# Moving keys and Gram products forward in the first layer of a delta-rule and feed-forward kernel

## The chip, the cores and the metric

The kernel runs on one core of a Trainium2 chip. A core has a matrix engine (TensorE, PE in the profile; its weight loads are PEld), a vector engine (VectorE, DVE), a scalar engine (ScalarE, ACT), a general engine (GpSimd, POOL) and a queue engine (SyncE, SP), which here only issues DMA transfers. Each engine works through its own list of instructions in order and waits on semaphores for the others. The metric is the device time of one execution in microseconds.

## The reference

Two parts follow one another. The first is a delta rule over 768 tokens, for 4 batches of 8 heads with 48 dimensions: for each token

```
k_n   = k / (|k| + 1e-6)
y_t   = q_t . state                      (before the update)
v_old = state . k_t
state = state + beta_t * outer(k_t, v_t - v_old)
```

The second takes the outputs as 3072 rows `x` of 384 and computes

```
h = x @ w_in                             (384 to 2048)
g = max(h, 0) + alpha * min(h, 0)
out = g @ w_out                          (2048 to 384)
```

All of it is in 32-bit floating point. The inputs are q, k, v, beta, w_in, w_out and alpha; the only output is `out`.

## The kernel before

The 768 tokens are cut into 12 chunks of 64, and the 4 batches into 2 pairs. One chunk of one pair is a *step*; there are 24 steps, numbered 0 to 23, with two steps per chunk. A step holds 128 rows (2 batches of 64 tokens) and 8 heads. Within a chunk, the rule becomes matrix products: the products of all keys with one another (the *Gram* products, `grams`, L486), a triangular system, products with the state, and an update of the state. The triangular inverses of four steps are made together on DVE by an elimination (`eliminate`: four block transposes L540, one mask on POOL L555, then 30 steps of two instructions each, L565 and L571, and transposes back). `eliminate(1)` does this for steps 4 to 7, and can start when the four Gram products of these steps have been weighed (L494) and copied into one tile (`keep`, L529).

When both steps of a chunk are done, its 256 tokens go through the feed-forward part: `ffn_in` (L1075) multiplies by w_in, 48 products of 128x256 per chunk; six products make a pair of column blocks in one of two PSUM banks, which ACT (L1085) and DVE (L1087) then evict. `ffn_out` (L1118) multiplies by w_out. PE's whole list is written out by hand as an interleaving: `weave` deals out the steps of generators by their shares, `alongside(p, c)` puts p products of `ffn_in(0)` and c half conversions of weights between two pieces of the attention part.

The weights arrive as 32-bit words and are converted before use. Each piece takes two instructions on ACT (L240, L242), a shift on DVE (L256) and an addition on POOL or DVE (L263). w_in comes in 12 pieces of 512 KB, w_out in 16 pieces of 384 KB, through staging areas in tiles that have other uses later. `weights()` holds the bookkeeping: `fetch(n)` issues loads until n pieces have been issued; when a piece is finished, the conversion fetches one more. ACT begins the conversion of the next piece before the current one is finished. All loads go through SP's queue in the order of the program, together with the loads of keys, queries and values (L137, L175). A load into a tile waits in that queue until the readers of the tile are done.

`pause(n, upto)` (L1664) puts a one-element memset on POOL into a staging area, and then fetches: the load has to wait for the memset, and so for everything that POOL has in its list before it. Two such pauses delay parts of w_in.

In the first layer, steps 0 to 3 are handled specially. `first_chunk` does steps 0 and 1, with an elimination in small blocks. Before it, some matrix products whose results are not used (`busy`, L1539, 5.5 products of 128x512) stand in PE's list; they write a PSUM bank that was read just before by the copies of the masked query products (`a_t`, L1569 on ACT). `second_pair` then does steps 2 and 3: the products with the inverses (`own_values` and three calls of `one_round`, L857), the outputs (L930), and the state update (L946), woven with `ffn_in(0)`. In between, it prepares steps 4 to 7: `keys(k)` transposes the keys of step k on PE (L430), copies them (`k_t`, L439), squares and sums them (L386, L393), and issues the load of the keys three steps further, which reuses the tile; `weigh` makes the weights from the norms (L408, L409, L413, L419, L420); `grams` makes the Gram products.

For the state update, `copy_late(n)` keeps a second copy of the keys of steps 0 to 3 with the two batches swapped for odd heads, in three instructions (L153, L155) on POOL.

Numbers that the text uses: `BEGUN` is the number of pieces of `eliminate(1)` that are done within `second_pair`, `SOON` the number done in the next weave; the rest follows while `ffn_out(0)` runs.

Of the kernel before, what the change touches and what calls it, by code (L numbers as in the profile page):

```python
# [25 lines left out]
FP32 = mybir.dt.float32  # L26
# [17 lines left out]
def kernel(  # L44
# [11 lines left out]
    nc = tc.nc  # L56
# [8 lines left out]
    G = H // 2  # L65
# [38 lines left out]
    def half(i):  # L104
        return slice(64 * i, 64 * i + 64)
# [39 lines left out]
    def late_key(n):  # L145
        return late_keys.get(n, k_late[n % NKL])

    def copy_late(n):

        if n >= NKL:  # L150
            late_keys[n] = work.tile([128, DM], FP32, name="o_sb").rearrange("p (h d) -> p h d", h=H)
        src, dst = (x.rearrange("p (g a) d -> p a g d", a=2)[:, :, :, 0:D] for x in (early(n), late_key(n)))
        nc.gpsimd.tensor_copy(out=dst[:, 0], in_=src[:, 0])  # L153
        for t in range(2):
            nc.gpsimd.tensor_copy(out=dst[half(1 - t), 1], in_=src[half(t), 1])  # L155

    def load_q(n):
        if n < N:
# [2 lines left out]
    def load_v(n):  # L161
        if n < N:
            v_raw[n] = work.tile([128, H, D], FP32, name="v_raw", bufs=3)
            fetch(v, n, v_raw[n])
# [301 lines left out]
    def now(pieces):  # L466
        for x in pieces:
            x()
# [1193 lines left out]
    def pause(n, upto):  # L1662

        nc.gpsimd.memset(in_stages[n][0:1, 0:1].bitcast(FP32), 0.0)  # L1664
        fetch_in(upto)
# [3 lines left out]
    for f in range(FT // 2, FT, 2):  # L1669
        stages.append(w_out[:, f : f + 2].rearrange("p f d -> p (f d)").bitcast(U32))  # L1670
    ids = [0, 1, 2, 3, 4, 5, 6, 0, 1, 2, 6, 0, 1, 2, 0, 1]
    fetch_out, _, conv_out = weights(pieces, stages, ids, out_done, None, 5, 1)
    PARTS_OUT = 2 * len(pieces)

# [17 lines left out]
    def gram(n):  # L1692
        return grams(n, big[n % 3])

    for n in (0, 2, 3):
        copy_late(n)
    squared(0)
    copy_0 = key(0)
# [31 lines left out]
    first_weights(1)  # L1730
    for c in range(2):
        first_spread(c, quarter_weight, quarter_of, NQ4)
    copy_late(1)
    gram_3 = gram(3)
    pick(3, gram_3, 0)
    picks(2, gram_2)
# [9 lines left out]
    raw(2, gram_2)  # L1746
    raw(3, gram_3)
    nc.scalar.mul(minus, minus, -1.0)
    load_v(2)
    for n in range(1, NJ):  # L1750
        load_early(n + NKE)
    load_v(3)
    mask = queries(big[1])
    slopes()
    short(5, ps_one())
# [16 lines left out]
    def alongside(products, pieces, *gens):  # L1772
        gens = [(part(first_in, products), products), (part(convert_on, pieces), pieces), *gens]
        weave(*[x for x in gens if x[1] > 0])

    def second_pair():

        n, m, x = 2, 3, NJ
        both = (n, m)

        def burst(step, width):
            p = ps_big()
            pieces = []
            for i in range(2):
                pieces += step(n + i, p[:, :, i * width : (i + 1) * width])
            now(pieces)

        def keys(k):
            flip_more(k)
            squared(k)  # L1790
            norms(k)
            load_early(k + NKE)

        def through(i, p):
            now(through_state(i, None, p))

        now(next_state(0))
        scale_first(n)
        pause(8, 10)
        scale_first(m)  # L1800
        alongside(2, 2)
        now(next_state(1))
        keys(x)
        alongside(3, 3)
        burst(matrix, G * C)
        for i in both:
            turn_matrix(i, nc.gpsimd)
        now(weigh(x))
        alongside(3, 2)
        for i in both:  # L1810
            flips(N, i)
            load_q(i + 2)
        fetch_in(11)
        alongside(2, 1)
        keys(x + 1)
        fetch_in(12)
        alongside(2, 1)
        y = ps_big()
        through(n, y[:, :, 0 : G * D])
        alongside(2, 1)  # L1820
        through(m, y[:, :, G * D : 2 * G * D])
        now(weigh(x + 1))
        alongside(3, 2)
        burst(own_values, G * D)
        for i in both:
            turn_values(i, nc.gpsimd)
        fetch_out(1)
        alongside(3, 2)
        now(grams(x))
        alongside(2, 2)  # L1830
        burst(lambda i, p: one_round(i, 0, p), G * D)
        load_v(4)
        fetch_out(2)
        alongside(2, 1)
        keys(x + 2)
        fetch_out(3)
        alongside(2, 2)
        burst(lambda i, p: one_round(i, 1, p), G * D)
        now(weigh(x + 2))
        alongside(2, 1)  # L1840
        now(grams(x + 1))
        alongside(2, 1)
        burst(lambda i, p: one_round(i, 2, p), G * D)
        alongside(2, 1)
        keys(x + 3)
        fetch_out(4)
        alongside(2, 1)
        now(grams(x + 2))
        now(weigh(x + 3))
        alongside(2, 1)  # L1850
        burst(outputs, G * D)
        alongside(3, 2)
        now(grams(x + 3))
        alongside(2, 1)
        for i in both:
            to_ffn(i)
        squares(x + 4)
        alongside(2, 1, (part(blocks, 5), 5))
        for i in both:
            now(next_state(i))  # L1860
            load_late(i + 2)
            load_v(i + 3)
            alongside(2, 0)
        alongside(IN_PARTS - 45, 0)

    def flip_more(n):
        now(flipped(n, ps_one()))

    blocks, BEGUN, SOON, LAST = eliminate(1), 5, 9, 6
    second_pair()  # L1870
    weave(
        (part(conv_out, PARTS_OUT - 10 - LAST), PARTS_OUT - 10 - LAST), (ffn_in(1), IN_PARTS - 4),
# [166 lines left out]
```

## Time and profile before

| quantity | value |
|---|---|
| time, median of 3 runs | 653.72 us (652.72 to 653.98) |
| time of the profiled execution | 652.53 us |
| its span, first to last instruction | 650.8 us |
| DVE, ACT, POOL busy | 74%, 40%, 19% of the span |
| PE busy in 30 to 40, 40 to 50, 50 to 60 us | 8.35, 10.00, 8.62 us |
| PE busy in 60 to 70, 70 to 80, 80 to 90 us | 9.21, 10.00, 7.98 us |
| DMA engines' share in 50 to 60 us | 0.85 |

A row of the timeline gives the start, the duration, the engine, the line of the kernel, the operation, what it writes and reads, the sizes, and how many instructions were merged. In brackets stands how long the engine had been idle before it, and who released it; "issue" means that the profile shows nothing that it waited for. SPq rows are DMA issues; the transfer lands some microseconds later. In the chain of waits each row is a start, a duration and what took it.

### The profile page before, as it was taken

The page shows a single profiled execution, that of the slowest core. Times are in us where ns is not written, and L with a number is a line of the kernel's source. Part 1 is how long each engine was busy: PE and PEld are TensorE (multiplying, and loading weights), DVE is VectorE, ACT ScalarE, POOL GpSimd, SP SyncE. Part 2 cuts the span into 40 slices and gives each one's busy share as a digit, 9 for nine tenths or more (in the row PEclk, how much of TensorE's full clock was granted, in tenths as well). Part 3 has the DMA queues.
Part 4 walks back from the last instruction along what each step waited for, and adds up shares of the span by engine and source line. Part 5 has one row for each costly group of instructions (what it writes and reads, how often), then busy time and mean ns, then how long its engine had stood idle before and what let it go on. Part 6 is the DMA issues. An engine that isn't in the chain of part 4 may idle for free.

```text
span 650.8 us, 21349 instructions
## 1 busy us (share of the span) xinstructions
PE 633.3 (97%) x9157; PEld 559.0 (86%) x9157; DVE 483.4 (74%) x1157; ACT 258.2 (40%) x605; POOL 126.0 (19%) x250
## 2 busy tenths in 40 slices
PE   6998989999999999999999999999999999999997
PEld 5676777566789989989989989989999999999997
DVE  5857698978998788577678568678868568477383
ACT  6676565154645153154145144033145154042240
POOL 7296511010001000000000010000044053062350
PEclk9999999999999999999999999999999999999999
DMA  8856764013412320211211111121121210100000
GB/s 159 223 166 146 195 163 108 12 39 63 84 30 39 69 40 19 56 40 32 46 30 26 39 39 26 35 42 25 39 44 21 50 26 2 38 3 3 24 1 25
DMA packets 106798, 36.88 MB, mean 57 GB/s; under 512 B 99872, under 2 KB 103088, under 8 KB 106704
## 3 DMA queue, kind: packets, MB, share of 16 engines
q1 hardware_dynamic: 104832, 35.03, 24.2%
q8 instruction: 72, 1.18, 0.7%
q10 hardware_dynamic: 1872, 0.49, 0.4%
q14 instruction: 22, 0.18, 0.1%
HBM read 30.78 MB, written 4.72 MB: 55 GB/s over the span
## 4 chain that ended last, share of the span: by engine, by line
PE 85%; DVE 6%; DMA 3%; ACT 3%; issue 1%; SPq 1%; POOL 0%; ACTq 0%
PE p_ffn L1075 22%; PE p_ffn L1140 17%; PE p_more L1392 8%; PE p_more L1308 5%; PE p_ffn L1118 4%; PE p_ffn L1298 3%; PE p_ffn L1392 3%; PE p_ffn L1303 2%; PE p_pair L807 2%; PE p_pair L430 2%; PE p_pair L747 2%; PE p_pair L930 2%; PE p_pair L917 2%; PE p_pair L795 1%; PE p_pair L486 1%
## 5 line engine op out<-in xcount | busy, mean ns | idle before, releaser
L1075 PE MATMUL p_ffn<-xt,w_in 128*128 128x256 f32 x768 | 178.1, 384 | 2.6 <-DVE act L1087 2.4
L1075 PEld LDWEIGHTS p_ffn<-xt,w_in 128*128 128x128 f32 x768 | 141.7, 190 | 23.4 <-ACT space_out L242 2.3
L1087 DVE SCALAR_TENSOR_TENSOR act<-act,al_t,p_ffn 128x256 f32<-128x256 f32 x112 | 48.6, 475 | 22.7 <-ACT act L1085 22.5
L1085 ACT ACTIVATE act<-p_ffn 128x512 f32<-128x512 f32 x56 | 33.3, 595 | 79.8 <-PE p_ffn L1075 79.6
L1332 POOL TENSOR_TENSOR k_t<-k_t 128x128 f32<-128x128 f32 (+1 forms) x48 | 29.3, 610 | 167.2 <-ACT k_t L1327 164.7
L571 DVE TENSOR_TENSOR block<-block,prod 128x30 f32<-128x30 f32 (+9 forms) x150 | 49.9, 332 | 5.2
L419 POOL TENSOR_TENSOR beta_t<-beta_t,rec 128x8 f32<-128x8 f32 x20 | 5.1, 257 | 237.6 <-DVE rec L413 228.0
L565 DVE TENSOR_TENSOR prod<-block 128x30 f32<-128x30 f32 (+9 forms) x150 | 48.8, 325 | 2.8 <-POOL block L555 1.4
L1140 PE MATMUL p_ffn<-w_out,act 128*128 128x192 f32 x288 | 49.6, 328 | 0.0
L1140 PEld LDWEIGHTS p_ffn<-w_out,act 128*128 128x128 f32 x288 | 46.6, 190 | 0.3
L973 ACT COPY xt<-p_pair 128x384 f32<-128x384 f32 x22 | 10.4, 478 | 90.7 <-PE p_pair L969 76.9
L1332 POOL TENSOR_TENSOR block<-block 128x128 f32<-128x128 f32 (+1 forms) x48 | 27.9, 582 | 16.9 <-ACT block L1327 14.4
L1298 PE MATMUL p_ffn<-xt,w_in 128*128 128x256 f32 x96 | 28.7, 381 | 0.5 <-DVE o_sb L1160 0.5
L759 ACT COPY inv<-p_pair 32x256 f32<-32x256 f32 x40 | 14.5, 361 | 24.9 <-DVE u L921 24.1
L1160 DVE TENSOR_TENSOR o_sb<-u,p_ffn 128x192 f32<-128x192 f32 x24 | 7.9, 351 | 20.8 <-PE p_ffn L1140 20.0
L1346 DVE SCALAR_TENSOR_TENSOR act<-block,al_t,act 128x256 f32<-128x256 f32 x32 | 19.1, 637 | 5.3 <-ACT block L1342 5.3
L799 ACT COPY y<-p_pair 128x384 f32<-128x384 f32 x22 | 10.6, 480 | 30.8 <-PE p_pair L795 29.2
L825 DVE TENSOR_TENSOR r<-v_raw,p_pair 64x192 f32<-64x192 f32 (+1 forms) x60 | 21.1, 352 | 1.0
L1392 PE MATMUL p_more<-w_out,act 128*128 128x192 f32 x128 | 21.8, 329 | 0.0
L1327 ACT COPY k_t<-p_more 128x512 f32<-128x512 f32 x16 | 9.4, 586 | 31.4 <-PE p_more L1308 26.7
L1346 DVE SCALAR_TENSOR_TENSOR act<-k_t,al_t,act 128x256 f32<-128x256 f32 x32 | 21.7, 718 | 0.1
L807 PE MATMUL p_pair<-beside,k_t 48*64 48x112 f32 x704 | 21.4, 259 | 0.2 <-ACT beside L458 0.2
(287 smaller groups left out, 1409.0 us busy)
## 6 DMA issues: line engine op xcount, KB each, us to landing
v_raw<-in_v_dram SPq DMA_DIRECT2D x48, 96.0 KB, 2.9
qp<-in_q_dram SPq DMA_DIRECT2D x48, 96.0 KB, 3.0
out_dram<-o_sb SPq DMA_DIRECT2D x90, 48.0 KB, 1.6
space_out<-in_moe_w_out_dram SPq DMA_DIRECT2D x11, 384.0 KB, 3.9
ke<-in_k_dram SPq DMA_DIRECT2D x43, 96.0 KB, 3.1
kl<-in_k_dram SPq DMA_DIRECT2D x80, 48.0 KB, 2.6
w_out<-in_moe_w_in_dram SPq DMA_DIRECT2D x6, 512.0 KB, 7.6
w_out<-in_moe_w_out_dram SPq DMA_DIRECT2D x5, 384.0 KB, 6.0
```

Source lines behind the costliest of these rows:

```text
L565: nc.vector.tensor_tensor(out=prod, in0=r[:, 0:j, j : j + 1].to_broadcast([128, j, n]), in1=r[:, j : j + 1, j + 1 : HB].to_broadcast([128, ...
L571: nc.vector.tensor_tensor(out=r[:, 0:j, j + 1 : HB], in0=r[:, 0:j, j + 1 : HB], in1=prod, op=ALU.add)
L807: nc.tensor.matmul(p[half(t ^ a), a, g], k_t[n][dims(a), g, half(t)], beside[bp][dims(a), t, g])
L1075: nc.tensor.matmul(p_h[:, i], w_in[:, t, (f + i) * 128 : (f + i + 1) * 128], xt[:, t], start=(t == 0), stop=(t == KT - 1),)
L1085: nc.scalar.activation(g, p_h, ACT.Relu, scale=-1.0)
L1087: nc.vector.scalar_tensor_tensor(out=g[:, i], in0=g[:, i], scalar=al_t[:, f + i : f + i + 1], in1=p_h[:, i], op0=ALU.mult, op1=ALU.add,)
L1140: nc.tensor.matmul(p, x(i), w(i), start=(i == 0), stop=(i == FP - 1))
L1298: nc.tensor.matmul(p[:, f * 256 : f * 256 + 256], w(2, f), xt[:, 2], start=True, stop=False)
L1308: nc.tensor.matmul(q[:, j], a, b, start=True, stop=True)
L1332: nc.gpsimd.tensor_tensor(out=dst, in0=a, in1=b, op=ALU.add)
L1346: nc.vector.scalar_tensor_tensor(out=g[:, f], in0=r[:, f], scalar=al_t[:, 2 * i + f : 2 * i + f + 1], in1=g[:, f], op0=ALU.mult, op1=ALU.add,)
L1392: nc.tensor.matmul(p, x(i), w(i), start=(i == 0), stop=(i == FP - 1))
```

## The change

Six things change, all in the first 90 us.

- The second copies of keys 3 and 1 are made by ACT, after the sign change of `minus` and ahead of the copies of a_t. Those of 0 and 2 stay on POOL.
- As a consequence, the loads of keys 5 and 6 go ahead of the load of key 4, which follows the values of step 3.
- The second pause of w_in fetches up to 11 pieces instead of 10, and the last piece (12) is fetched where the 11th was.
- In `second_pair`, the Gram products of steps 4 to 7 and `keys` of steps 6 and 7 stand one or two stages earlier in PE's list, each stage being `own_values`, a round, or the outputs. The number of ffn products between them changes so that the total is the same.
- The loads of w_out's pieces start later: the first two are issued after the weights of step 6, behind a third pause (`pause_out`).
- Twelve pieces of `eliminate(1)` are done in `second_pair` instead of five, in four places, the first of them ahead of the outputs. `SOON` goes from 9 to 8.

```diff
-    def copy_late(n):
+    def copy_late(n, engine=nc.gpsimd):
...
-        nc.gpsimd.tensor_copy(out=dst[:, 0], in_=src[:, 0])
+        copy_by(engine, dst[:, 0], src[:, 0])
         for t in range(2):
-            nc.gpsimd.tensor_copy(out=dst[half(1 - t), 1], in_=src[half(t), 1])
+            copy_by(engine, dst[half(1 - t), 1], src[half(t), 1])
...
+    out_stages = stages
+    def pause_out(n, upto):
+        nc.gpsimd.memset(out_stages[n][0:1, 0:1].bitcast(FP32), 0.0)
+        fetch_out(upto)
...
-    for n in (0, 2, 3):
+    for n in (0, 2):
         copy_late(n)
...
-    copy_late(1)
     gram_3 = gram(3)
...
     nc.scalar.mul(minus, minus, -1.0)
+    for n in (3, 1):
+        copy_late(n, nc.scalar)
     load_v(2)
-    for n in range(1, NJ):
+    for n in (2, 3):
         load_early(n + NKE)
     load_v(3)
+    load_early(1 + NKE)
...
-        pause(8, 10)
+        pause(8, 11)
...
-        fetch_in(11)
+        fetch_in(12)
         alongside(2, 1)
         keys(x + 1)
-        fetch_in(12)
...
         now(weigh(x + 1))
-        alongside(3, 2)
+        alongside(2, 1)
+        now(grams(x))
+        alongside(2, 2)
         burst(own_values, G * D)
         for i in both:
             turn_values(i, nc.gpsimd)
-        fetch_out(1)
-        alongside(3, 2)
-        now(grams(x))
+        alongside(2, 1)
+        keys(x + 2)
+        alongside(2, 2)
+        now(grams(x + 1))
         alongside(2, 2)
         burst(lambda i, p: one_round(i, 0, p), G * D)
+        now(weigh(x + 2))
+        pause_out(0, 2)
         load_v(4)
-        fetch_out(2)
         alongside(2, 1)
-        keys(x + 2)
+        keys(x + 3)
+        alongside(2, 1)
+        now(grams(x + 2))
+        alongside(2, 1)
+        burst(lambda i, p: one_round(i, 1, p), G * D)
+        now(weigh(x + 3))
         fetch_out(3)
-        alongside(2, 2)
-        burst(lambda i, p: one_round(i, 1, p), G * D)
-        now(weigh(x + 2))
         alongside(2, 1)
-        now(grams(x + 1))
+        now(grams(x + 3))
         alongside(2, 1)
         burst(lambda i, p: one_round(i, 2, p), G * D)
-        alongside(2, 1)
-        keys(x + 3)
         fetch_out(4)
-        alongside(2, 1)
-        now(grams(x + 2))
-        now(weigh(x + 3))
-        alongside(2, 1)
+        alongside(3, 2, (part(blocks, 4), 4))
         burst(outputs, G * D)
-        alongside(3, 2)
-        now(grams(x + 3))
-        alongside(2, 1)
+        alongside(4, 3, (part(blocks, 1), 1))
         for i in both:
             to_ffn(i)
         squares(x + 4)
-        alongside(2, 1, (part(blocks, 5), 5))
+        alongside(2, 1, (part(blocks, 3), 3))
         for i in both:
             now(next_state(i))
             load_late(i + 2)
             load_v(i + 3)
-            alongside(2, 0)
-        alongside(IN_PARTS - 45, 0)
+            alongside(2, 0, (part(blocks, 2), 2))
+        alongside(IN_PARTS - 47, 0)
...
-    blocks, BEGUN, SOON, LAST = eliminate(1), 5, 9, 6
+    blocks, BEGUN, SOON, LAST = eliminate(1), 12, 8, 6
```

In `second_pair`, `x` is 4, so `keys(x + 2)` belongs to step 6 and `grams(x)` to step 4.

## The prediction

> **What bounds the kernel now.** First the page: TensorE (PE) is busy for 97% of the span, so time is won or lost only where PE sits idle, or where its order is held back.
>
> ```profile
> span 650.8 us, 21349 instructions
> PE 633.3 (97%) x9157; PEld 559.0 (86%) x9157; DVE 483.4 (74%) x1157; ACT 258.2 (40%) x605; POOL 126.0 (19%) x250
> ```
>
> Second, the waits of PE up to 200 us, because the diff ends at about 90 us and PE's order after that is unchanged. Two of them lie inside the edited stretch:
>
> ```profile
> PE p_pair L857 <- issue: 2.4, 3, 1.4
> PE p_ffn L1075 <- DVE act L1087: 2.4, 2, 1.9
> ```
>
> Third, the timeline of PE where they are. The first two stop in the middle of a burst, with no releaser; the third waits for VectorE (DVE), whose transposes and state updates (rows below it) are queued ahead of the eviction L1087.
>
> ```profile
> 54.59 0.56 PE L857 MATMUL p_pair<-r,diag 64*64 64x48 f32 x24 [0.79 <-issue]
> 60.79 0.26 PE L857 MATMUL p_pair<-sums 64*64 64x48 f32 x2 [1.38 <-issue]
> 87.00 5.42 PE L1075 MATMUL p_ffn<-xt,w_in 128*128 128x256 f32 x24 [1.92 <-DVE act L1087]
> ...
> 81.58 2.31 DVE L540 STREAM_TRANSPOSE block<-same 128x256 f32<-128x256 f32 x4
> 83.76 2.20 DVE L954 TENSOR_TENSOR beside<-beside,p_pair 48x384 f32<-48x384 f32 x4
> 85.98 0.87 DVE L1087 SCALAR_TENSOR_TENSOR act<-act,al_t,p_ffn 128x256 f32<-128x256 f32 x2
> ```
>
> Fourth, ScalarE (ACT) in the same stretch. Its queue is in order, and a conversion whose w_out piece has not landed (L240) stops all behind it:
>
> ```profile
> 63.10 0.54 ACT L386 ACTIVATE ksq<-ke 128x384 f32<-128x384 f32 x1
> 63.53 0.57 ACT L240 ACTIVATE w_out<-space_out 128x384 uint32<-128x384 uint32 x1
> ...
> 68.75 0.56 ACT L240 ACTIVATE w_out<-space_out 128x384 uint32<-128x384 uint32 x1 [2.76 <-DMA space_out<-in_moe_w_out_dram]
> 69.22 0.59 ACT L1085 ACTIVATE act<-p_ffn 128x512 f32<-128x512 f32 x1
> ...
> 78.54 0.56 ACT L240 ACTIVATE w_out<-w_out 128x384 uint32<-128x384 uint32 x1 [3.97 <-DMA w_out<-in_moe_w_out_dram]
> ```
>
> Fifth, the chain: a piece that stands behind a key load on the queue of SyncE (SP) lands 3.74 us after its issue.
>
> ```profile
> 64.31 0.63 SPq L137
> ...
> 64.99 3.74 DMA space_out<-in_moe_w_out_dram
> ```
>
> Before, these waits hit ACT while PE had other work. Last, the start, where `busy` keeps PE waiting for ACT's two copies of a_t:
>
> ```profile
> 19.18 1.12 ACT L1569 COPY a_t<-p_pair 128x512 f32<-128x512 f32 x2
> 20.35 7.39 PE L1539 MATMUL p_pair<-qp,ident 128*128 128x512 f32 x12 [0.37 <-ACT a_t L1569]
> 30.48 1.57 ACT L871 COPY act<-act 64x192 f32<-64x192 f32 x4
> ```
>
> **The change part by part.** Times are on the clock of the trace before, unless I say otherwise.
>
> *Late keys by ACT.* Six copies leave POOL (which waits there anyway, so nothing is won) and stand on ACT between `minus` and a_t. L871 takes 0.35 to 0.41 us each: 6 x 0.36 = 2.2 us. a_t ends at 22.5, not 20.3; `busy` fills PE from its start for 7.39 us, and the first product of the first chunk follows it directly (27.67). ACT's 5.0 us of idle time up to 28.44 hides its own conversions, but not PE's. Everything up to 38.5 hangs on that product, and after it PE is full to 53.8, so nothing absorbs the shift: **+2.2**. Bounds: L1539's pieces start 0.85 us apart until 24.78 and 0.43 after 25.43. If the doubling stays at its moment, 3.2 of 12 pieces run slow: end at 29.0, +1.3. [...]
>
> *Key loads on SP.* Key 4 (ke_78) is loaded last of three, behind v, and must await ACT's copy. It goes out near 28 instead of 18.03, lands within its 3.1 us, and is needed at 40.18 (+2.2). q slips by 1.3 us of issue, needed at 44.5. Nothing. Pieces 10 and 11 of w_in go out earlier (sums near 41, not 47.87); both land before ACT wants them. Nothing.
>
> *Products and keys moved forward.* The same matmuls, in new places: Gram 4 before `own_values`, keys 6 and Gram 5 before round 0, keys 7 and Gram 6 before round 1, Gram 7 before round 2. From 51.58 I add rows: two ffn products 1.06 (0.86 after a flip), a Gram burst 0.62, a flip 0.44, a round 1.07. own_values runs 54.3 to 55.6, round 0 59.6 to 60.7 (before, 61.05 with two stalls), round 1 64.7 to 65.9. The two issue stalls are 24+6+32+4+62 = 128 matmul records apart, and the instruction queue q8 has its packets at 51.9 and 58.4 beside data transfers that fill 85% of the engines. With w_out's pieces away, I take them as gone but for 0.2: -2.0. [...]
>
> *Third pause.* `pause_out(0, 2)` puts a 1x1 memset on POOL ahead of w_out's first two loads. In POOL's order it stands behind L420 of key 6, which needs DVE's reciprocal, which stands behind round 0's sums; and behind four more conversions (L263, 1.3 each), two pairs of swaps and two of `keep`. Added up from 54.6, when Gram 4 is weighed: `keep` 0.9, L263 1.3, swaps 1.5, L263 2.6, `keep` 0.9, L263 1.3, weights 0.5: memset at 63.7, against loads at 51.19 and 53.61 before. The very next conversion in program order wants piece 0: ACT, done with the roots of key 6 at 60.9, **waits for it to 67.4** (63.7 + 3.7). Bounds of a landing: 2.9 to 3.9, the minimum and median of the loads into space_out. 3.74 is the nearest row.
>  Behind that L240 on ACT stand L242, L240 of piece 1, the copy of k_t 7 and its square. So k_t 7 comes at 69.5, and PE, ready for Gram 7 at 66.9, waits 2.7.
>  Then the second wait. `fetch_out(3)` and `(4)` find as many pieces fetched already, so the lead is two pieces, not three, and piece 2 stands on SP behind keys(7)'s reload of ke_78, which must await the square (70.0): two issues of 0.63, piece 2 at 71.3, landed at 75.0. In ACT's order its L240 comes *ahead* of L1085, the eviction of ffn pair 5; L1087 of that pair stands on DVE ahead of round 1's sums; round 2 needs those. 75.0 + 0.5 + 0.6 + 0.05 + 0.85 + 0.6: **round 2 starts at 77.6**; PE was free at 71.1. Bounds of this landing: 2.9, and 6.0 (the later w_out row of the chain).
>
> *Elimination moved forward* (BEGUN 5 to 12). After round 2, `outputs` runs 80.4 to 81.9. Ahead of `y` DVE now has all four transposes (0.56 each) and an eviction, so to_ffn waits from 83.6 to 84.8. The rest of PE's list ends at 90.6 (82.3 before), and five products later, at 93.2, PE wants the bank of the last ffn pair. Its L1087 stands behind seven steps of elimination (0.4 to 0.7 each, 4.0 by the rows from 89.95 on) and four L954 (2.2), and ends at 95.1. So the 1.92 us stall isn't removed, it has another cause. 95.2 against 87.0: **+8.2** for this stretch, the -2.0 included.
>
> *Rest of the weave.* PE is full from 87 to 133; DVE, 90 to 96% busy there, has six steps less later. PE idles 0.8 us in 140 to 200, of which I take -0.3 (bounds -0.8, and +2 if the shorter lead makes ACT wait there too).
>
> **Sum.** 2.2 + 8.2 - 0.3 = +10.1 us. The profiled execution took 652.53 (span 650.8 and 1.7 around it): 662.6. It lies 1.2 below the median of three, 653.72, so for a median 663.8, and I say **664**. Bounds added: -0.9 - 0.8 - 0.8 - 0.5 = 661 below, +0.8 + 0.2 + 2.3 + 2.3 = 669 above.
>
> **Rivals.**
> *No wait (other side).* The pieces are at hand when ACT asks. For it: the same engine list without waits ends at 79.8, 2.5 before the old end, and the last bank is then free near 82.9 instead of 87.0; with +2.2 and -0.3 that is -2.2, 651.5. Against: the memset cannot come before round 0's sums (62.5), and landing takes 2.9 at least. It decides if both landings together cost PE under about 2 us.
> *Half.* Only the first wait reaches PE, because piece 2 lands while PE is still behind. Then 664 less about 6 is 658. Against: its issue hangs on the square that the first wait delays.
> *The array slows down in the gap.* PE idles 71.1 to 77.6. After the start it ran at half rate for 4.4 us of unbroken work; the same again costs up to 2.2, of which the wait for `y` hides 1.2: 665 to 666. No gap after 28 us in this trace exceeds 2 us, so no row shows it. [...]
> *Change without effect*: order on four engines changes, so only by cancelling.
>
> **Chances.** As summed 0.55 (661 to 669), slowed array 0.17 (663 to 670), half 0.12 (655 to 661), no wait 0.11, within 0.2% (1.3 us, about what a measurement tells) by cancelling 0.03, worse still 0.02. Slower 0.86. The range 655 to 670 leaves out no wait, no change and the worst.
>
> **What would show it.** After: L1539 starts near 22.5; L857 has no issue wait over 0.3; ACT's L240 waits for space_out twice, 4 to 7 us and 4 to 5 us; PE waits for k_t at a Gram burst (2 to 3 us) and for r at L857 (5 to 7 us); the first L1075 run of 24 starts near 97. It is wrong if ACT shows no such waits between 60 and 80, or if L1085 of pair 5 is released without the DMA.

## The result and the profile after

The changed kernel takes 668.5 us (median of 6 runs, 665.21 to 669.41); the kernel before, run beside it, 653.22 us (6 runs, 650.98 to 653.98). The ratio is 1.0234, with a 95% interval from 1.0206 to 1.0263: slower by 15.3 us. The forecast was 664, in a range from 655 to 670. The profiled execution took 669.41 us, so it is 0.9 above its median; 1.7 of it lies outside the span.

The page's first lines show the span 16.9 us longer, with PE busy 5.8 us more (633.3 before). The products are the same, so some of them ran slower, and the remaining 11 us are idle time of PE:

```profile
span 667.7 us, 21348 instructions
...
PE 639.1 (96%) x9157; PEld 564.0 (84%) x9157; DVE 483.4 (72%) x1157; ACT 260.3 (39%) x611; POOL 123.6 (19%) x245
```

PE's waits up to 200 us (what PE wanted, what it waited for; total, number and longest in us):

```profile
PE p_pair L486 <- ACT k_t L439: 5.4, 1, 5.4
PE p_pair L857 <- DVE r L912: 5.2, 2, 5.0
...
PE p_pair L1539 <- ACT a_t L1569: 2.4, 1, 2.4
PE p_ffn L1075 <- ACT w_out L240: 2.2, 1, 2.2
PE p_pair L857 <- ACT w_in L240: 1.1, 1, 1.1
PE p_pair L930 <- issue: 0.7, 1, 0.7
```

The first two are new, and they are the waits for k_t and for r that the prediction named. The two issue stalls in own_values and round 0 are not in the list any more. Two rows carry a name that misleads: the 2.2 us ahead of L1075 stand under L240, which ends within 0.1 us of the eviction that L1075 needs (DVE's L1087, at 101.18 below), and the 1.1 us ahead of L857 are a stall of the kind that shift_block explains. The timeline of all engines from 67 us shows where the first two waits come from:

```profile
67.61 0.09 POOL L1676 MEMSET space_out<- 1x1 f32 x1
67.73 0.81 SPq L223 DMA_DIRECT2D space_out<-in_moe_w_out_dram  x2
...
73.09 0.54 ACT L240 ACTIVATE w_out<-space_out 128x384 uint32<-128x384 uint32 x1 [9.60 <-DMA space_out<-in_moe_w_out_dram]
...
74.55 0.57 ACT L439 COPY k_t<-p_pair 112x512 f32<-112x512 f32 x1
...
75.17 1.13 PE L486 MATMUL p_pair<-k_t 48*64 48x64 f32 x32 [5.38 <-ACT k_t L439]
...
75.56 1.29 SPq L137 DMA_DIRECT2D ke<-in_k_dram  x2
...
76.89 0.62 SPq L223 DMA_DIRECT2D space_out<-in_moe_w_out_dram  x1
...
80.82 0.55 ACT L240 ACTIVATE w_out<-space_out 128x384 uint32<-128x384 uint32 x1 [4.83 <-DMA space_out<-in_moe_w_out_dram]
81.27 0.58 ACT L1085 ACTIVATE act<-p_ffn 128x512 f32<-128x512 f32 x1
...
81.88 0.87 DVE L1087 SCALAR_TENSOR_TENSOR act<-act,al_t,p_ffn 128x256 f32<-128x256 f32 x2 [4.83 <-ACT act L1085]
...
82.67 0.54 DVE L912 TENSOR_TENSOR r<-act,p_pair 128x384 f32<-128x384 f32 x1
```

Read downwards, this is one chain, with PE's row hanging on it at the side. The memset releases piece 0; ACT stands 9.6 us until it has landed; only then does ACT copy k_t 7, for which PE has been idle 5.4 us. The square behind that copy lets SP reload ke_78 at 75.56; piece 2 is issued behind it, lands 3.9 us later, and holds up ACT again, and with it L1085, L1087 and the sums. Round 2 starts at 83.27.

What follows the two waits runs at a lower clock: it falls within the first wait, at 72.68, and is back at 89.74. The windows of that stretch (start, end and length in us; the busy time of PE, PEld, DVE, ACT and POOL; then the granted clock, the DMA share and GB/s):

```profile
72.68:89.74 17.06, 9.60 (x170) 7.49 (x170) 8.80 (x22) 8.04 (x18) 5.59 (x10) 0.50 0.64 162
89.74:103.40 13.66, 11.43 (x126) 9.28 (x119) 11.37 (x32) 6.72 (x16) 3.42 (x5) 1.00 0.45 120
99.99:103.40 3.41, 1.21 (x6) 1.11 (x7) 3.29 (x11) 2.02 (x4) 0.40 (x1) 1.00 0.51 144
103.40:106.81 3.41, 3.41 (x10) 2.70 (x9) 2.41 (x7) 0.28 (x1) 0.21 (x1) 0.50 0.18 43
```

And PE's own timeline there, with rows that have a twin at full clock elsewhere (six L1075 1.56, 64 of L930 1.15, a run of 24 5.42), and the eviction that the last of them waits for:

```profile
85.16 2.93 PE L1075 MATMUL p_ffn<-xt,w_in 128*128 128x256 f32 x6
88.02 1.91 PE L930 MATMUL p_pair<-u,a_t 64*64 64x48 f32 x64
...
101.18 0.87 DVE L1087 SCALAR_TENSOR_TENSOR act<-act,al_t,p_ffn 128x256 f32<-128x256 f32 x2
...
102.19 7.11 PE L1075 MATMUL p_ffn<-xt,w_in 128*128 128x256 f32 x24 [2.23 <-ACT w_out L240]
```

That run of 24 ends at 109.3. Before, it ended at 87.00 + 5.42 = 92.42. The difference, 16.9, is that of the spans: on balance all of the loss has happened by then, and nothing is given back later.

### The profile page after: what moved, and what is told of

Read it like the earlier page. It is cut to its first block, busy times and chain, and to the rows that moved or that the text cites. A ratio compares the mean times of both kernels' runs of the same rounds, so it can differ in the third digit from the quotient of the medians.

```text
span 667.7 us, 21348 instructions
## 1 busy us (share of the span) xinstructions
PE 639.1 (96%) x9157; PEld 564.0 (84%) x9157; DVE 483.4 (72%) x1157; ACT 260.3 (39%) x611; POOL 123.6 (19%) x245
## 4 chain that ended last, share of the span: by engine, by line
PE 86%; DVE 6%; ACT 4%; DMA 2%; issue 1%; POOL 1%; SPq 0%; ACTq 0%; DVEq 0%
PE p_ffn L1075 23%; PE p_ffn L1140 17%; PE p_more L1392 8%; PE p_more L1308 4%; PE p_ffn L1118 4%; PE p_ffn L1298 3%; PE p_ffn L1392 3%; PE p_ffn L1303 2%; PE p_pair L430 2%; PE p_pair L807 2%; PE p_pair L930 2%; PE p_pair L747 2%; PE p_pair L486 2%; PE p_pair L917 2%; DMA space_out<-in_moe_w_out_dram 1%; PE p_pair L946 1%
## 5 line engine op out<-in xcount | busy, mean ns | idle before, releaser
L1075 PE MATMUL p_ffn<-xt,w_in 128*128 128x256 f32 x768 | 182.3, 390 | 2.8 <-ACT w_out L240 2.2
L1075 PEld LDWEIGHTS p_ffn<-xt,w_in 128*128 128x128 f32 x768 | 144.6, 194 | 24.3 <-ACT w_out L240 2.6
L1087 DVE SCALAR_TENSOR_TENSOR act<-act,al_t,p_ffn 128x256 f32<-128x256 f32 x112 | 48.6, 475 | 25.9 <-ACT act L1085 25.7
L1085 ACT ACTIVATE act<-p_ffn 128x512 f32<-128x512 f32 x56 | 33.4, 597 | 81.7 <-PE p_ffn L1075 81.5
L1332 POOL TENSOR_TENSOR block<-block 128x128 f32<-128x128 f32 (+1 forms) x48 | 27.7, 577 | 16.7 <-ACT block L1327 14.2
L1298 PE MATMUL p_ffn<-xt,w_in 128*128 128x256 f32 x96 | 28.7, 381 | 0.5 <-DVE o_sb L1160 0.5
L486 PEld LDWEIGHTS p_pair<-k_t 48*64 48x64 f32 x768 | 15.3, 152 | 9.6 <-ACT k_t L439 5.8
L486 PE MATMUL p_pair<-k_t 48*64 48x64 f32 x768 | 18.2, 241 | 5.4 <-ACT k_t L439 5.4
L954 DVE TENSOR_TENSOR beside<-beside,p_pair 48x384 f32<-48x384 f32 (+1 forms) x38 | 20.9, 549 | 1.7 <-PE p_pair L946 1.4
```

What stands on the lines that cost most here:

```text
L486: nc.tensor.matmul(p[own, a, g], k_t[n][dims(a), g, half(t)], k_t[n][dims(a), g, half(t)])
L1075: nc.tensor.matmul(p_h[:, i], w_in[:, t, (f + i) * 128 : (f + i + 1) * 128], xt[:, t], start=(t == 0), stop=(t == KT - 1),)
L1085: nc.scalar.activation(g, p_h, ACT.Relu, scale=-1.0)
L1087: nc.vector.scalar_tensor_tensor(out=g[:, i], in0=g[:, i], scalar=al_t[:, f + i : f + i + 1], in1=p_h[:, i], op0=ALU.mult, op1=ALU.add,)
L1298: nc.tensor.matmul(p[:, f * 256 : f * 256 + 256], w(2, f), xt[:, 2], start=True, stop=False)
L1332: nc.gpsimd.tensor_tensor(out=dst, in0=a, in1=b, op=ALU.add)
```

## The experiments

All ratios are to the kernel before, run on the same chip beside each group. 1% is 6.5 us.

| kernel | what it is | median, us | ratio (95%) |
|---|---|---|---|
| the change | | 668.5 | 1.0234 (1.0206 to 1.0263) |
| early_out | w_out fetched early again | 657.15 | 1.0068 (1.0045 to 1.0090) |
| pause_three | lead of three pieces | 661.23 | 1.0128 (1.0083 to 1.0173) |
| no_memset | no memset, lead of two | 661.85 | 1.0163 (1.0136 to 1.0191) |
| pool_keys | copies back on POOL | 665.03 | 1.0192 (1.0144 to 1.0240) |
| after_begun5 | elimination as before | 663.4 | 1.0184 (1.0159 to 1.0210) |
| warm_gap | unused products in the gaps, too many | 670.89 | 1.0278 (1.0238 to 1.0318) |
| warm_gap2 | the same, as many as fit | 666.36 | 1.0213 (1.0168 to 1.0258) |
| act_keys_alone | before, copies by ACT | 653.84 | 1.0028 (1.0005 to 1.0050) |
| moved_only | early w_out, copies on POOL | 653.95 | 1.0026 (1.0005 to 1.0047) |
| moved_begun5 | the same, elimination as before | 650.92 | 0.9982 (0.9954 to 1.0010) |
| moved_again | moved_begun5, more runs | 651.61 | 0.9985 (0.9969 to 1.0000) |
| shift_block | before, 24 records more | 651.46 | 0.9988 (0.9970 to 1.0006) |

My theory was that of the prediction, enlarged by its third rival: w_out's late pieces stop ACT, ACT stops PE twice, and the array slows down in the gaps. The rivals were that the elimination, or the copies by ACT, cost most.

### early_out: the whole change, but w_out fetched early

```diff
+        fetch_out(1)          # after turn_values, behind own_values
...
-        pause_out(0, 2)
         load_v(4)
+        fetch_out(2)
...
+        fetch_out(3)
         keys(x + 3)
...
         now(weigh(x + 3))
-        fetch_out(3)
```

> Everything of the change is kept but the late start of w_out: its pieces are fetched from the places between own_values and round 1 again, one, two and three ahead, with no memset before them. Theory (late pieces stop ACT, ACT stops PE twice, and the array slows in the two gaps): both waits of ACT in 60 to 85 us go, PE waits neither for k_t nor for r, the run of 24 products takes about 5.4 us again, and of the 15.3 us that the change cost, 3 (keys by ACT) stay, perhaps 1 to 2 of the elimination: 653 to 658. Rival A (the elimination that was moved ahead costs most): over 662. Rival B (the copies by ACT and the later first chunk cost most): over 662 with no wait for L240 left. The issue stalls of PE (0.8 and 1.4 us) come back if the fetches cause them.

It measured 1.0068: 1.66% under the change, so the late fetch alone makes about 10.8 of the 15.3 us. Theory's range holds, and both rivals fall as the largest part. PE's timeline:

```profile
69.38 0.69 PE L486 MATMUL p_pair<-k_t 48*64 48x64 f32 x32
...
71.82 0.68 PE L857 MATMUL p_pair<-r,act 64*64 64x48 f32 x32 [0.68 <-DVE r L912]
...
78.85 1.01 PE L969 MATMUL p_pair<-ident,y 128*128 128x128 f32 x6 [1.09 <-DVE y L936]
...
89.50 5.42 PE L1075 MATMUL p_ffn<-xt,w_in 128*128 128x256 f32 x24 [2.18 <-DVE act L1087]
```

The Gram burst of step 7 waits for nothing, and r costs 0.7 instead of 5.0. The wait of 2.2 us ahead of the run of 24 remains. One thing came out otherwise than I had thought: w_out's first piece is fetched at 53.9, ahead of own_values as in the kernel before, and yet the issue stalls in own_values and round 0 stay away. That speaks against the loads of w_out as their cause; shift_block, below, asks what it is.

### pause_three and no_memset: the two waits, one at a time

```diff
-        pause_out(0, 2)
+        pause_out(0, 3)       # pause_three
...
-        pause_out(0, 2)
+        fetch_out(2)          # no_memset
         load_v(4)
```

> The change with one number different: the third pause fetches three pieces instead of two, so piece 2 stands on SP right behind pieces 0 and 1 and ahead of the reload of ke_78. Theory: piece 0 still lands at about 73, the first wait (5.4) stays; piece 2 lands 75 to 76 instead of 80.8, so round 2 starts 4 to 5 us earlier and the array cools less: 668.5 less 5 to 8, 660.5 to 663.5. Rival (the second wait only takes over what round 2 would wait for on DVE or POOL anyway): 667 to 669.

> The change with the third pause replaced by the plain call that issues pieces 0 and 1 at the same place in the program; the one-element memset on POOL is gone, the lead of two stays. Theory (the memset, deep in POOL's order, is what makes piece 0 late; the lead of two makes the second wait): SP issues piece 0 near 62 instead of 67.7, it lands near 66, k_t 7 is ready before PE wants it at 70, and the first gap goes; piece 2 still stands behind the reload of ke_78, issued near 71, so round 2 waits until 77 to 78 instead of 83.3, with some rows at half rate behind it: 668.5 less 4.5 to 7, 661.5 to 664. Rival (the transfer itself, 5.3 us here, makes both waits, wherever it is issued): 667 to 669.

Both medians lie in the theory's ranges, and each kernel loses just one of the two waits. In pause_three, ACT and PE:

```profile
72.26 0.54 ACT L240 ACTIVATE w_out<-space_out 128x384 uint32<-128x384 uint32 x1 [8.80 <-DMA space_out<-in_moe_w_out_dram]
...
75.47 0.54 ACT L240 ACTIVATE w_out<-space_out 128x384 uint32<-128x384 uint32 x1
```

```profile
74.76 1.14 PE L486 MATMUL p_pair<-k_t 48*64 48x64 f32 x32 [5.00 <-ACT k_t L439]
...
77.94 1.11 PE L857 MATMUL p_pair<-r,act 64*64 64x48 f32 x32
...
95.67 7.10 PE L1075 MATMUL p_ffn<-xt,w_in 128*128 128x256 f32 x24 [2.18 <-ACT w_out L240]
```

The first wait is whole, and piece 2 (75.47) is there when ACT comes to it: round 2 waits for nothing. One piece more of lead is worth 1.06% of the time. In no_memset it is the other way round (SP's issues, then PE):

```profile
61.29 1.04 SPq L223 DMA_DIRECT2D space_out<-in_moe_w_out_dram  x2
...
70.85 0.63 SPq L223 DMA_DIRECT2D space_out<-in_moe_w_out_dram  x1
```

```profile
69.13 0.69 PE L486 MATMUL p_pair<-k_t 48*64 48x64 f32 x32 [0.46 <-ACT k_t L439]
...
77.16 1.10 PE L857 MATMUL p_pair<-r,act 64*64 64x48 f32 x32 [6.27 <-DVE r L912]
```

Without the memset the pieces leave 6.4 us earlier, the first gap shrinks to 0.5, and the second, which the lead of two makes, grows to 6.3.

### pool_keys and act_keys_alone: the copies by ACT

pool_keys is the change with the copies of keys 3 and 1 on POOL, and with the key loads in their old order; act_keys_alone is the kernel before with only this part of the diff. The edit of pool_keys (that of act_keys_alone is its reverse):

```diff
-    for n in (0, 2):
+    for n in (0, 2, 3):
         copy_late(n)
...
+    copy_late(1)
     gram_3 = gram(3)
...
-    for n in (3, 1):
-        copy_late(n, nc.scalar)
     load_v(2)
-    for n in (2, 3):
+    for n in range(1, NJ):
         load_early(n + NKE)
     load_v(3)
-    load_early(1 + NKE)
```

> The change with the copies of keys 3 and 1 given back to POOL and the key loads in their old order; everything else stays. Theory (the copies cost what the trace shows at the first L1075 and the second L795, 2.6 to 3.0 us, all kept to the end, as PE's later waits hang on PE's own earlier work): 668.5 less 2.5 to 3.5, 665 to 666. Rival (the copies cost nothing in the end, the waits for w_out absorb them): 668 to 669.

> The kernel before with one part of the change: keys 3 and 1 copied by ACT, and the loads of keys 5 and 6 ahead of key 4. Theory (these copies delay a_t, the first product and all that PE does after it, and nothing later takes the delay up): the first L1075 1.5 to 2.7 us later, and all of it kept: 652.6 plus 1.5 to 3, 654 to 655.6. Rival (PE's wait for L1087 at 85 us and the two issue stalls take it up): 652 to 653.

pool_keys is 0.42% under the change (about 2.7 us; its median lies at the lower end of the theory's range), and so are moved_only and early_out apart, which also differ only in this. Alone, the copies cost 0.28% (1.8 us): in the profile, PE's run of 24 starts at 87.95, 0.95 later than before, because the wait ahead of it shrinks from 1.92 to 0.76 and takes up a part. The median, 653.84, lies between the ranges of the theory (from 654) and of its rival (to 653), so both missed; it is nearer to the theory, though the interval (0.05 to 0.50%) is wide.

### moved_only and moved_begun5: the products, and the elimination

moved_only is early_out and pool_keys together, so it has nothing of the diff but the moved products and keys and the twelve pieces of elimination. moved_begun5 has the elimination back as well:

```diff
-        alongside(3, 2, (part(blocks, 4), 4))
+        alongside(3, 2)
         burst(outputs, G * D)
-        alongside(4, 3, (part(blocks, 1), 1))
+        alongside(4, 3)
...
-        alongside(2, 1, (part(blocks, 3), 3))
+        alongside(2, 1, (part(blocks, 5), 5))
...
-            alongside(2, 0, (part(blocks, 2), 2))
+            alongside(2, 0)
...
-    blocks, BEGUN, SOON, LAST = eliminate(1), 12, 8, 6
+    blocks, BEGUN, SOON, LAST = eliminate(1), 5, 9, 6
```

> The change without its late start of w_out and without the copies by ACT: what is left is the Gram products and keys moved forward, and twelve pieces of elimination ahead. Theory: early_out less what the copies cost, 657.1 less 2 to 3.5, 653.5 to 655; the two issue stalls stay away (2.2 us won), and the wait for y (1.1), for u and r (0.9) and for L1087 (2.2), which early_out shows, eat that up. Rival A (the move is worth its 2.2 us): 650 to 651.5. Rival B (the move of the products costs time of its own): over 655.5.

> moved_only with the elimination as in the kernel before: five pieces in second_pair, nine in the next weave. Theory (the seven elimination steps and the early transposes on DVE make the waits for y and for L1087): L1087 of the last pair ends about 3 us earlier against PE, the wait of 2.2 us goes or falls under 0.8, the wait for y falls under 0.5: moved_only less 2 to 3, 650.5 to 652.5. Rival (the wait for L1087 comes from the two pairs of L954 and the L1075 that are closer together at the end of second_pair): moved_only within 0.7 us.

moved_only measured 1.0026 (653.95 us, within its theory's range), moved_begun5 0.9982: about 2.9 us apart, as the theory has it. The rows of moved_only, and behind them those of moved_begun5:

```profile
76.62 1.01 PE L969 MATMUL p_pair<-ident,y 128*128 128x128 f32 x6 [1.55 <-DVE y L936]
...
87.26 5.42 PE L1075 MATMUL p_ffn<-xt,w_in 128*128 128x256 f32 x24 [2.17 <-ACT w_out L240]
```

```profile
79.69 1.01 PE L969 MATMUL p_pair<-ident,y 128*128 128x128 f32 x6 [0.17 <-DVE y L936]
...
88.36 5.42 PE L1075 MATMUL p_ffn<-xt,w_in 128*128 128x256 f32 x24 [0.20 <-DVE act L1087]
```

The wait for y falls from 1.55 to 0.17 and the one ahead of the run of 24 from 2.17 to 0.20. Both come from DVE: the transposes stand ahead of `y`, and seven steps of elimination ahead of the last L1087 (from 86.24 to 87.11 in moved_only, where the row gives L240 for it). (The start times of the two profiles are not compared. This one of moved_begun5 took 653.99 us, the longest of its ten runs; it lost some 4 us in the first chunk, where the granted clock was 0.50 from 38.28 to 45.11. moved_again, the same program, lost less there.)

### after_begun5: the elimination, with the late fetch kept

The same edit as in moved_begun5, made in the change itself.

> The change with only the elimination put back: five pieces in second_pair, nine in the next weave. Theory (twelve pieces make the wait for the last bank, 2.2 us, and let the array slow down in it, 1.7 us for the run of 24 products; both add to the waits for w_out): 668.5 less 2.5 to 4, 664.5 to 666. Rival (the waits for w_out give DVE time for the elimination, so it costs nothing here): 668 to 669.

663.4: 0.50% under the change by the ratios, 5.1 us by the medians; the theory's range began at 664.5, so the elimination costs more here than I had written. The rival falls: the waits for w_out do not hide the elimination. PE's timeline shows the wait gone, and the run of 24 at full clock:

```profile
97.66 5.42 PE L1075 MATMUL p_ffn<-xt,w_in 128*128 128x256 f32 x24 [0.26 <-DVE act L1087]
```

### warm_gap and warm_gap2: the slow array by itself

The change, with products added in the two gaps that read fixed data and that nobody reads:

```diff
         fetch_out(3)
-        alongside(2, 1)
+        alongside(3, 1)
+        fill(20)              # 10 in warm_gap2
         now(grams(x + 3))
-        alongside(2, 1)
+        fill(18)              # 14 in warm_gap2
+        alongside(1, 1)
...
+    def fill(n):
+        for _ in range(n):
+            nc.tensor.matmul(ffn_banks[turn[0]][:, 256:512], ident, w_in[:, 0, 0:256])
```

> The change with 38 products more, 128x256 of fixed data, whose results nobody reads: 20 ahead of the Gram products of step 7 and 18 behind them, 4.3 and 3.9 us at the warm rate of 0.215 us, in the two gaps in which PE waits. They take nothing away and add no wait. Theory (cooling is a cost of its own): the waits for k_t and r stay where they are, but the products behind them run at full rate: round 2 in 1.1 instead of 2.0 us, the run of six L1075 in 1.6 instead of 2.9, the run of 24 in 5.4 instead of 7.1; 668.5 less 3 to 5, 663.5 to 665.5. Rival (the slow rows are something else, DMA or a throttle): the same slow rows, 668 to 670.

> As warm_gap, with 10 products before the Gram products of step 7 and 14 behind them, priced by what warm_gap showed: 0.44 us for a product, not 0.215 (a product is two records), so 4.4 and 6.2 us, inside the waits of 5.4 and of 7.0 us (what the second becomes when the Gram products before it run warm). Nothing is taken away and no wait is added. Theory (the slow array costs time of its own): r for round 2 still comes at about 83, and from there round 2 takes 1.1 instead of 2.0, six L1075 1.6 instead of 2.9, L930 1.15 instead of 1.91: 3.0 us less, 665.5; 663.8 if the run of 24 products is at full rate too. Rival (the rows after the waits are slow for another reason, or DVE sets the pace there): 668 to 669.

warm_gap missed because I had priced a record as a product. PE's timeline counts two matmul records for each product in 32-bit floating point:

```profile
68.68 8.80 PE L1788 MATMUL p_ffn<-w_in,ident 128*128 128x256 f32 x40
```

20 products (40 records) took 8.80 us, not 4.3, and ran 3.4 us past the gap. warm_gap2 has the right number; its rows:

```profile
83.60 0.68 PE L857 MATMUL p_pair<-r,act 64*64 64x48 f32 x32 [0.61 <-DVE r L912]
...
90.59 1.01 PE L969 MATMUL p_pair<-ident,y 128*128 128x128 f32 x6 [1.06 <-DVE y L936]
...
101.24 7.11 PE L1075 MATMUL p_ffn<-xt,w_in 128*128 128x256 f32 x24 [2.17 <-ACT w_out L240]
```

Round 2 and the products behind it run at full clock (the 32 records at 0.68 us, 1.11 in the change), so the slow rows do come from the gaps. But from the start of round 2 to the run of 24 it is 17.6 us instead of 18.9: only 1.3 of the 3.0 us arrive, because a wait for y takes the place of slow products. The medians are 2.1 us apart, and their intervals overlap. The run of 24 is as slow as in the change (7.11 us), though the gaps are filled; the wait of 2.17 us just ahead of it is still there (the last section says in which profiles such a wait goes with a slow run). Two of the four runs, at a mean granted clock of 0.999 and 1.00, took 665.57 and 666.27 us, so some 666 us remain of this kernel even with next to no work at half rate.

### shift_block: what the issue stalls are

Summing the counts of PE's rows from the start, every issue stall up to 61 us in the profile of before follows record 473, 600, 981 or 1109. These lie 127, 381 and 128 apart: one or three times 128 records, but for a missing record or two. The instruction queue q8 has packets at 30.0, 33.7, 51.9 and 58.4, and PE goes on 2.4 to 2.7 us after each. At each of them PE is 54 to 84 records into the 128 that end at the stall. From these four rows I estimated that a stall comes where the rest of the 128 runs in less than about 2.5 us, and nowhere else. own_values and round 0 are such places in the kernel before: 40 and 62 records into a burst of short products. To test it, the kernel before gets 24 records more, of the same total width:

```diff
-BUSY = 5.5
+BUSY = 17.6
...
-            x = p[:, 0 : int(512 * min(n, 1))]
+            x = p[:, 0 : round(160 * min(n, 1))]
```

> The kernel before with the unused products of L1539 cut into 18 of 160 columns instead of 6 of 512: the same columns, 24 matmul records more, so all that follows stands 24 records later in PE's list. Theory (PE stalls where a block of 128 matmul records ends, at records 473, 600, 981 and 1109 of every run so far, and only if its last 60 or so records run in less time than the next block takes to come, 2.4 us from its packet): the stalls stay at these counts and so move in the program; the one of own_values falls ahead of the burst, behind six L1075, and goes to under 0.3 us; the one of round 0 comes 38 records into the burst and shrinks from 1.4 to 0.3 to 0.6; those of the first chunk move and stay at 0.3 to 1.2 each. 651 to 652.5. Rival (loads of w_out and keys keep the queue busy): 0.8 and 1.4 us stay where they are, 40 and 62 records into their bursts.

```profile
33.06 1.02 PE L857 MATMUL p_pair<-act 64*64 64x48 f32 x52 [1.24 <-issue]
...
36.75 1.02 PE L930 MATMUL p_pair<-u,a_t 64*64 64x48 f32 x53 [0.63 <-issue]
...
54.04 1.15 PE L857 MATMUL p_pair<-r,diag 64*64 64x48 f32 x64
...
58.80 0.29 PE L857 MATMUL p_pair<-sums 64*64 64x48 f32 x6
59.42 0.61 PE L857 MATMUL p_pair<-sums 64*64 64x48 f32 x26 [0.33 <-issue]
...
85.95 7.10 PE L1075 MATMUL p_ffn<-xt,w_in 128*128 128x256 f32 x24 [1.94 <-DVE act L1087]
```

The stalls stay at records 473, 600 and 1109 and move in the program by 24: after 38 records of round 0 instead of 62, 0.33 us instead of 1.38. own_values runs through. The loads of w_out's first pieces stand where they stood in the program, around own_values (53.1 and 55.0). The rival falls. The total shows no clear gain (0.12% less, interval from -0.30 to +0.06%). In the profile the first chunk's two stalls are 1.24 and 0.63 here, against 0.24 and 0.44, and the run of 24 took 7.10 instead of 5.42; both vary between profiles, so they do not settle where the gain of the other runs went.

### moved_again: the version that might beat both

> moved_begun5 once more, with more rounds: products and keys moved forward, w_out fetched early, copies on POOL, elimination as in the kernel before. Theory: the two issue stalls (2.2 us) are won, the wait for r ahead of round 2 (1.1 us) takes half of it: 0.1 to 0.3% under the kernel before. Rival: no difference, within 0.1%.

0.9985, with an interval from 0.9969 to 1.0000. Together with moved_begun5 (0.9982) it points to a gain of 1 us, and the interval just reaches no gain.

```profile
span 649.4 us, 21345 instructions
...
PE 633.6 (98%) x9157; PEld 558.9 (86%) x9157; DVE 482.9 (74%) x1157; ACT 257.9 (40%) x605; POOL 125.8 (19%) x250
```

### The sum of the parts

By the ratios, taking the parts away from the change in one order: products and keys moved -0.17% (-1.1 us, mean of moved_begun5 and moved_again), elimination +0.43% (+2.8), copies by ACT +0.42% (+2.7), late fetch of w_out +1.66% (+10.8): together the 2.34%, as they must, being steps from the change to moved_begun5 and from there to the kernel before. Each step has an uncertainty of some 2 us. Elimination and copies have a second pair each that agrees (0.50% from after_begun5, 0.42% from pool_keys); the fetch is far outside it.

## Why the prediction was right, and where it was off

**The mechanism was right.** The two waits are where the prediction put them, with the instructions it named behind each, and two edits showed that the memset makes the first and the lead of two pieces the second. The change came out slower, inside the range with 1.5 us to spare, 4.5 us above the forecast.

**Late keys by ACT: +2.2, measured 1.8 to 2.7.** The lower bound, +1.3, holds. The 0.8 that the upper sum adds to the 2.2 is shown by no run: in the eight profiles with the copies on ACT the first product starts between 28.34 (the change) and 29.89 (pause_three), 0.7 to 2.2 later than in the kernel before. In the profile of the change the way was different: `busy` ran 6.41 us instead of 7.39, so the first product came only 0.7 later (28.34), and PE lost the rest behind it, 1.15 instead of 0.24 at record 473 and some products at a clock of 0.50 from 38.5 to 42.0 us. The first L1075 starts 2.6 later. But that is one profile, and with the copies on POOL the stall at record 473 also reaches 1.06 (pool_keys). In the eight profiles with the copies on ACT the first product starts at 29.1 on average, in the six with them on POOL at 27.7, and the first L1075 at 40.9 against 39.4: 1.5 later both times. So the mechanism is the prediction's, and by the profiles near its lower bound; that this one profile comes out at 2.6, close to 2.2, is luck.

**The issue stalls: gone, but not for the reason given.** "With w_out's pieces away, I take them as gone" is the step that failed: they go with the pieces fetched early as well. What the runs show is a spacing of 128 records, which the prediction had seen. In shift_block, where six L1075 (1.56 us) and then only 16 short records of own_values stand ahead of that count, there is no stall; where the last 38 or more are short ones, PE stood 0.24 (the kernel before, record 473) to 1.66 us (act_keys_alone, record 1109). Of the -2.0, about -1.1 is left for the moved products as a whole, because round 2 then waits 0.8 to 1.1 us for r (moved_again 0.78, moved_begun5 1.11).

**Third pause and second wait: too small.** Put on the clock of after (+2.2), the memset was forecast at 65.9 and stood at 67.6; the landing was taken as 3.7 us, within bounds of 2.9 to 3.9, and took 5.3 from SP's issue. So piece 0 came at 73.0 instead of 69.6, and the second wait, which hangs on the first, passed that on: round 2 at 83.3 instead of 79.8. Here the mechanism held and the terms were mis-sized, by 1.7 and 1.6 us. The landing fell outside its bounds, which were the least and the median of the loads into that tile: a bound from the median leaves half of the rows out. The nearest rows were others: the loads of these same two pieces in the trace of before (51.19 and 53.61), issued among others, took 7.5 and 6.6 us to land. So the two signs of the first wait were too small as well: ACT waited 9.6 us for piece 0 where the prediction named 4 to 7, and PE 5.4 for k_t where it named 2 to 3.

**Elimination: counted in one case and not in the other.** The prediction saw that L1087 would stand behind seven steps, and that is what the trace after shows, at 101.2. But the rival without waits was priced at 651.5 as if the last bank were free at 82.9; early_out, which is that case, took 657.15. Its run of 24 starts at 89.50, where the rival had 85.1 (82.9 and the 2.2 of the keys); the waits for r, `y` and L1087, 0.68, 1.09 and 2.18, make 3.9 of the 4.4. The elimination (2.8 us) was left out of that price, and it alone is more than the products win.

**The slowed array: a rival at 0.17, and it came true.** The clock fell earlier than it had it, in the first gap, after 2.9 us of idle time, and not in the second. Its price of up to 1.0 net (2.2 less the wait for `y`) is close to the 1.3 that warm_gap2 shows. What it did not have is the run of 24 behind the wait of 2.2 us, at 7.11 instead of 5.42. The prediction's sum ends where that run starts. The last section has five profiles in which a wait of this length cost nothing behind it, so in the profile it is bad luck.

**The rest** was taken as -0.3 and was nothing. In all, the profiled execution took 669.4 against 662.6 forecast for it: 3.5 of that at the start of round 2, 1.3 more up to the run of 24, 1.7 in it, 0.3 in the rest.

## What to carry to other kernels

Before a load is put later, ask which in-order engine meets its data first, and what of the critical engine stands behind that instruction; two such waits in a row add up, because the second load's issue can hang on work that the first one delayed. Count the lead in pieces for the same reason: one piece more was worth 1% here. And where work is put ahead on an engine that is off the critical path, look at every eviction behind it, in the case without the big wait as well.

## What the runs showed of the hardware that was not expected

- **Stalls at fixed counts.** In the first 61 us of the kernel before, PE stops after matmul records 473, 600, 981 and 1109, that is 127, 381 and 128 apart; shift_block and the other profiles have their stalls at the same counts, from 0.24 us (the kernel before, 473) to 1.66 us (act_keys_alone, 1109). In the traces of the kernel before and of the change, PE goes on 2.4 to 2.7 us after a packet on the instruction queue, and the packet comes 54 to 86 records into the 128 that end at the stall. It shows as "issue", or with the name of whatever happened to end then (L240 or L242 at record 473). Two profiles of one program, moved_begun5 and moved_again, have 1.06 and 0.94 us at record 473, and 1.26 and 0.72 at 600, and in the first of them four L1075 behind these stalls took 2.07 us instead of 1.13, at a granted clock of 0.50. That is a part of the spread of up to 6 us between runs of one kernel; I have not shown that it is all of it.
- **A wait of 2 us, and behind it 1.7 us lost or nothing.** Ten profiles have a wait of 1.92 to 2.23 us ahead of the same 24 records. Five ran them in 7.10 to 7.11 us (the change, pause_three, warm_gap, warm_gap2 and shift_block), five in 5.42 (early_out, pool_keys, moved_only, no_memset and the kernel before), with nothing in between. In the trace of the change the granted clock is 1.00 or 0.50, and a stretch at 0.50 in mid-kernel lasted 3.41 us or five times that: 3.41 from 38.54, 17.06 from 72.68 and 3.41 from 103.40. The starts lie ten and nine times 3.41 us apart. Laid on steps of that length, the wait in the change lies within one, from 99.99 to 103.40, and the clock is 0.50 in the next, which loses half of 3.41, 1.7 us. In pause_three, warm_gap and warm_gap2 the windows of 2 us from 92 to 108 add up to 3.4 us at 0.50 as well, beginning 0.6, 0.6 and 0.9 us behind the end of the wait, so that the 3.41 us ahead hold all of its 2.2. In early_out, where PE idles from 87.32 to 89.50, the end of a step divides the wait, and the clock stays at 1.00:

```profile
84.97:88.38 3.41, 2.35 (x12) 1.74 (x10) 3.16 (x9) 3.07 (x8) 0.00 (x0) 1.00 0.89 219
88.38:91.80 3.42, 2.30 (x11) 2.07 (x12) 3.37 (x11) 1.09 (x3) 0.61 (x2) 1.00 0.50 122
```

  The change's window from 99.99 to 103.40, above, has PE busy for 1.21 us, and the next one is at 0.50. That the place of the wait makes the difference is my reading of these five profiles; for the other five it was not shown. In the first chunk the clock also fell in three profiles (the change, moved_begun5, warm_gap2: four L1075 took 1.53, 2.07 and 2.07 us there instead of 1.13) with no wait over 1.3 us, among short products, so idle time is not all that counts there; what else does stays open.
- **Records and products.** A product in 32-bit floating point is two matmul records here; one of 128x256 took 0.44 us (warm_gap: 20 products, 40 records, 8.80 us), not the 0.215 I had priced.
